# A new instruction order for attention followed by an MLP: planner with margins, last pair's shared tile first, block 8 ahead of blocks 6 and 7, small additions on ScalarE

## The chip, the cores and the metric

The kernel runs on one NeuronCore of a Trainium2 chip. Its engines work through queues of their own, in order: PE (TensorE: matmuls, with weight loads on PEld), DVE (VectorE), ACT (ScalarE), POOL (GpSimd), and SP, which here only issues DMAs, transposes among them. An engine waits for others through semaphores. The metric is the device time of one execution in microseconds (us), lower is better; a time is the median of several runs.

## The reference

Attention with pooled queries over 4 batches x 8 heads, 1152 keys and 576 queries (pairs of neighbours averaged), head size 64; then an MLP over the 2304 rows of 512 features.

```python
q_pool = q.reshape(B, H, S // 2, 2, D).mean(axis=3)
scores = (1 / np.sqrt(D)) * q_pool @ k.transpose(0, 1, 3, 2)
attn = np.exp(scores - scores.max(axis=-1, keepdims=True))
attn = attn / (attn.sum(axis=-1, keepdims=True) + 1e-09)
x = (attn @ v).transpose(0, 2, 1, 3).reshape(B * S // 2, H * D)
h = x @ w_in
out = (h * (1 / (1 + np.exp(-1.702 * h)))) @ w_out
```

q, k and v arrive as 32-bit floats, the weights in double precision. Where the kernel works in f16, it splits an operand into a high and a low f16 part, so that one product becomes three f16 matmuls (high x high, high x low, low x high).

## The kernel before

Heads are worked on in 16 pairs, four to a batch. Each pair has nine tiles of scores (128 queries x 1152 keys): A0, A1, B0, B1, A2, A3, B2, B3 of its two heads, and a shared tile L that holds the last 64 queries of both. Tiles are numbered through, 0 to 143. The first four pairs (tiles 0 to 35) are worked on in 32-bit floats: PE transposes the exponentials (`w_tr`) and ACT or DVE evacuates them (`w_ev`). The other twelve run in f16, and these steps follow one another for a tile:

- `scores` on PE into the one score tile in PSUM (`s`, three banks, one buffer);
- `row_max` on DVE: negated copy into `p` (3 buffers) and row minimum `nm`;
- `lift` on DVE: adds 15 ln 2 to `nm` (so that the f16 parts don't underflow);
- `exps` on ACT: exp with bias `nm`, and the row sums into `w_d`;
- `p_hi` on ACT or DVE: f16 copy of `p` into `hl` (3 buffers);
- `p_lo` on POOL or DVE: the rest, `p` minus that copy;
- `p_tr` on SP: a DMA transpose of both parts into `pt`.

When the four tiles of a group (two of each head), or L, are there, `pv` on PE multiplies by v; `w_denom` on POOL adds 1e-9 to the sums, `w_recip` on DVE inverts, `w_rows` on PE and `w_spread` (ACT or DVE) spread them, `x_div` on DVE multiplies, `x_hi` and `x_lo` split the result for the MLP. A pair's q, k and v go through their own steps ahead (`q_add` on POOL, maxima, `q_hi`, `q_lo`, `k_hi`, `k_lo`, `v_hi`, `v_lo`, two transposes on SP). The weights are unpacked from double precision (`w_exp`, `w_low`, `w_bits`, `w_sign`, `w_mul`, then `w_hi`, `w_lo`) during the first pairs.

The MLP works in nine blocks of 256 rows: two to a batch (0 to 7) of the tiles A and B, and block 8 of the remaining rows, the L tiles of all pairs, prepared by `last_scale`, `last_hi` and `last_lo`. A block has eight steps: `moe_h` in four pieces of six matmuls (an "h piece") into one PSUM buffer, `moe_tanh` on ACT, `moe_gate` on DVE, `moe_hi` on ACT or DVE, `moe_lo` on DVE, and `moe_o` in four pieces of three matmuls (an "o piece"). A block ends with two evacuations (`out_ev` on ACT) and stores on SP.

The order in which instructions stand on the engines is made by a planner (class `Plan`): each task has an engine or several to choose from (`or_on`, by the table `movable`), a cost in us, a rank, and buffers that it takes and gives back. `order` goes through a simulated time; for each engine it looks for the tasks that can start within `wait` of the earliest one and takes that with the lowest rank. The numbers in `rank`, `wait` and `sizes` are set by hand in the source. What it emits stands as it is: an engine whose next instruction waits does nothing else. Tasks marked `two`, and POOL's, are kept apart by the planner (`lock`): they don't overlap in its time.

Of the kernel before, what the change touches and what calls it, by code (L numbers as in the profile page):

```python
# [23 lines left out]
class Plan:  # L24
# [12 lines left out]
    def __init__(self, sizes, wait):  # L37
        self.sizes, self.wait, self.tasks, self.users, self.takers = sizes, wait, [], {}, {}
# [22 lines left out]
    def order(self):  # L61
# [14 lines left out]
        def start(t, e):  # L76
# [4 lines left out]
            for tag, _ in t["take"]:  # L81
# [3 lines left out]
                if at >= 0:  # L85
                    key = held[at]
                    if pend[key]:
                        return None
                    s = max(s, ended[key])
            return s  # L90

        while len(out) < len(self.tasks):
# [13 lines left out]
            cost = t["on"][eng]  # L106
            if eng == "PE":
                cost += self.SWITCH * (t["mode"] != mode)
                mode = t["mode"]
# [16 lines left out]
            for h in heirs.get(t["name"], ()):  # L126
                for e in h["on"]:
                    at = free[e] if e == eng and (e == "PE" or h["name"][0] == t["name"][0]) else seen
# [10 lines left out]
def kernel(  # L139
# [45 lines left out]
        w1=1971.8069114113, w1_rate=22.2436521906, w2=2562.6136217615, w2_rate=0.1126475672,  # L185
        w1_cut=2729.3607183991, w1_cut_rate=0.2375636551, w2_cut=-194.4633781393, w2_cut_rate=0.0258145275,
        v_max=410.1342476678, load=-538.8306800934, prep=169.5826065521, max=-1414.4144022325,
        exp=-771.055026078, p_hi=-369.4985057232, p_lo=318.2880489272, pv=1732.7584590916, x=1798.622401704,
        recip=1777.4431451824, w_tr=1309.6396350423, w_ev=935.5365655987, g=-1469.0890297392,
        pv_b=-864.4518785428, max_b=1888.3689951722, p_lo_b=1106.2277461912, prep_b=-1313.6605845069,  # L190
        v=1427.6770251219, lift=-747.0450393382,
    )
    movable = dict(DVE=('x_hi', 'p_hi', 'x', 'w_hi', 'k_hi', 'moe_hi', 'q_hi', 'qk_ev'), POOL=('p_lo', 'w_exp'))
    wait = dict(PE=0.005839, ACT=0.318681, DVE=0.098398, POOL=1.168057)
# [4 lines left out]
    plan = Plan(sizes, wait)  # L199
# [25 lines left out]
    i_l = const.tile([128, 1], F32, name="i_l")  # L225

# [162 lines left out]
    ORDER = SLOTS  # L389
    pairs, tile_of, num = [], [], {}  # L390
    for P in range(NPAIR):
        pairs.append(Pair(P, len(tile_of), ORDER))
        for kind, t in ORDER:
# [290 lines left out]
    def w_denom(g, u):  # L684
        c = w_cols(g, u)
        nc.gpsimd.tensor_scalar(
            out=w_r[:, c], in0=w_d[:, c], scalar1=1e-9 * (1 if g.whole else 2 ** LIFT), scalar2=1.0, op0=ALU.add, op1=ALU.mult
# [6 lines left out]
    def lift(e, n):  # L694

        m = T["nm", n]
        (nc.vector if e == "DVE" else nc.gpsimd).tensor_scalar(  # L697
# [432 lines left out]
```

## Time and profile before

| | us |
|---|---|
| median of 3 runs (820.05 to 821.11) | 820.67 |
| the profiled execution | 818.89 |
| its span, first to last instruction | 817.1 |
| PE busy / DVE / ACT / POOL | 771.6 / 614.7 / 526.0 / 318.5 |

PE is busy 94% of the span, DVE 75%, ACT 64%, POOL 39%. The page cuts the span into 40 slices of some 20 us; a digit is the busy share in tenths:

```profile
PE   6999999999889898998899999998989999999997
DVE  5786999889999898887989698989788783222222
ACT  5887888988567776686578675656666753222222
POOL 3432334355536455353436664527564530000000
```

Three stages are seen: the first four pairs (to about slice 8), the twelve f16 pairs with MLP blocks between them, and from slice 34 on MLP blocks alone. An idle time of an engine is written behind an instruction with what ended it ("<-"), and a wait for several semaphores is put down to the one that came last.

### The profile page before, as it was taken

How to read it: one execution, taken by the hardware profiler on the slowest of the kernel's cores; microseconds unless marked ns; L12 is line 12 of the kernel's file. 1: busy time of each engine (PE TensorE's matmuls, PEld its weight loads, DVE VectorE, ACT ScalarE, POOL GpSimd, SP SyncE). 2: the span in 40 equal slices, each digit the busy share in tenths (PEclk: the TensorE clock that was granted, in tenths of full speed). 3: DMA queues.
4: the chain of work that ended last, by engine and by line, in shares of the span. 5: the costliest groups of instructions: out<-in, count | busy, mean ns of one | idle time of the engine just before them, and what ended most of it. 6: DMA issues, size and time to landing. Idle time of an engine off the chain costs nothing.

```text
span 817.1 us, 16805 instructions
## 1 busy us (share of the span) xinstructions
PE 771.6 (94%) x6756; PEld 515.6 (63%) x6756; DVE 614.7 (75%) x1053; ACT 526.0 (64%) x787; POOL 318.5 (39%) x235
## 2 busy tenths in 40 slices
PE   6999999999889898998899999998989999999997
PEld 3566666666656566666567666666666667666664
DVE  5786999889999898887989698989788783222222
ACT  5887888988567776686578675656666753222222
POOL 3432334355536455353436664527564530000000
PEclk9999999999999999999999999999999999999999
DMA  8554333769899999999999999999999981000001
GB/s 300 186 173 151 119 125 103 195 125 176 179 176 229 196 205 196 210 195 221 198 206 192 214 204 205 207 215 201 213 182 177 172 139 39 1 27 1 26 1 26
DMA packets 336142, 128.77 MB, mean 158 GB/s; under 512 B 311232, under 2 KB 321472, under 8 KB 336064
## 3 DMA queue, kind: packets, MB, share of 16 engines
q1 hardware_dynamic: 335776, 127.10, 74.6%
q8 instruction: 53, 0.87, 0.4%
q10 hardware_dynamic: 288, 0.59, 0.3%
q14 instruction: 25, 0.20, 0.1%
HBM read 45.09 MB, written 4.72 MB: 61 GB/s over the span
## 4 chain that ended last, share of the span: by engine, by line
PE 62%; DVE 18%; DMA 7%; issue 5%; ACT 4%; SPq 2%; POOL 1%; DVEq 0%; ACTq 0%; POOLq 0%
PE h L951 16%; PE o L987 14%; PE s L654 7%; DMA pt<-hl 6%; DVE p L668 5%; PE s L625 5%; PE pv L733 5%; PE o L745 5%; PE pv L768 5%; DVE kn L497 2%; PE h L308 2%; PE tr L780 2%; DVE hl L254 1%; ACT hl L252 1%; DVE hl L707 1%
## 5 line engine op out<-in xcount | busy, mean ns | idle before, releaser
L707 POOL TENSOR_TENSOR hl<-p,hl 128x1152 f16<-128x1152 f32 x85 | 210.6, 2480 | 186.1 <-ACT hl L252 121.5
L668 DVE TENSOR_SCALAR_CACHE_REDUCE p<-s,e_s 128x1152 f32<-128x1152 f32 x144 | 203.2, 1411 | 41.4 <-PE s L654 15.9
L675 ACT ACTIVATE p<-p,nm 128x1152 f32<-128x1152 f32 x144 | 180.0, 1250 | 56.8 <-DVE nm L697 41.5
L987 PE MATMUL o<-wbuf,g 128*128 128x512 f16 x864 | 205.1, 380 | 0.0
L951 PEld LDWEIGHTS <-wbuf 128*128 128x128 f16 x1728 | 167.5, 98 | 44.7 <-issue 10.1
L654 PE MATMUL s<-kT,qT 128*128 128x384 f16 (+1 forms) x720 | 125.6, 330 | 15.8 <-DVE p L668 15.8
L987 PEld LDWEIGHTS <-g 128*128 128x128 f16 x864 | 82.6, 98 | 85.6 <-issue 3.3
L252 ACT ACTIVATE hl<-p 128x1152 f16<-128x1152 f32 x84 | 97.1, 1157 | 40.6 <-DMA pt<-hl 29.8
L951 PE MATMUL h<-x16a,wbuf 128*128 128x256 f16 x960 | 118.5, 275 | 4.8 <-DVE gf L965 4.7
L959 ACT ACTIVATE th<-h,t_s 128x512 f32<-128x512 f32 x72 | 49.2, 684 | 103.9 <-PE h L951 103.7
L965 DVE SCALAR_TENSOR_TENSOR gf<-th,h 128x512 f32<-128x512 f32 x72 | 49.2, 683 | 85.6 <-ACT th L959 85.5
L654 PEld LDWEIGHTS <-qT 128*128 128x128 f16 (+1 forms) x720 | 63.2, 101 | 63.1 <-issue 25.9
L733 PEld LDWEIGHTS <-vhl 128*64 128x64 f16 x1944 | 80.9, 111 | 21.0 <-issue 17.3
L951 PE MATMUL h<-wbuf 128*128 128x256 f16 x768 | 91.9, 274 | 0.0
L733 PE MATMUL pv<-pt,vhl 128*64 128x256 f16 x1296 | 78.4, 274 | 2.0 <-DMA pt<-hl 2.0
L976 DVE SCALAR_TENSOR_TENSOR g<-gf,g 128x512 f16<-128x512 f32 x72 | 64.3, 894 | 20.0 <-ACT g L252 19.8
L252 ACT ACTIVATE g<-gf 128x512 f16<-128x512 f32 x55 | 34.4, 626 | 33.3 <-DVE gf L965 33.3
L303 POOL TENSOR_TENSOR wbuf<-raw 128x512 f32<-128x512 f32 x32 | 34.1, 1070 | 44.8 <-ACT raw L299 42.8
L745 PE MATMUL o<-idf,p 128*128 128x128 f32 x324 | 50.3, 283 | 0.4 <-ACT pt L252 0.2
L625 PE MATMUL s<-kT,qT 64*128 64x512 f32 (+3 forms) x240 | 49.3, 522 | 0.2 <-DVE p L668 0.2
L252 ACT ACTIVATE pt<-o 128x384 f32<-128x384 f32 x96 | 43.4, 483 | 8.8 <-PE o L745 8.2
L745 PEld LDWEIGHTS o<-idf,p 128*128 128x128 f32 x324 | 35.9, 141 | 17.9 <-issue 6.2
(104 smaller groups left out, 810.0 us busy)
## 6 DMA issues: line engine op xcount, KB each, us to landing
vraw<-in_v_dram SPq DMA_DIRECT2D x32, 288.0 KB, 3.4
kraw<-in_k_dram SPq DMA_DIRECT2D x30, 288.0 KB, 3.5
qraw<-in_q_dram SPq DMA_DIRECT2D x32, 256.0 KB, 4.0
raw<-in_moe_w_in_dram SPq DMA_DIRECT2D x16, 512.0 KB, 4.6
raw<-in_moe_w_out_dram SPq DMA_DIRECT2D x16, 512.0 KB, 4.8
out_dram<-osb SPq DMA_DIRECT2D x16, 256.0 KB, 2.7
pt<-hl SPq DMA_TRANSPOSE x96, 5.1
qraw<-in_q_dram SPq DMA_DIRECT2D x32, 32.0 KB, 3.6
```

What stands on the lines that cost most here:

```text
L252: nc.scalar.activation(out=out, in_=in_, func=ACTF.Copy, scale=1.0 if scale is None else scale)
L625: nc.tensor.matmul(out=ps[m, bank, 0:128 * (last - first)], lhsT=qT[h, (j - half) % NJ, m], rhs=kT[h, first:last].rearrange("p j c -> p (j ...
L654: nc.tensor.matmul(out=ps[m, c, 0:384], lhsT=st, rhs=T["kT", g.P][:, o:o + 3].rearrange("p r c -> p (r c)"), start=(l == 0), stop=(l == 1),)
L668: nc.vector.tensor_scalar(out=p, in0=s, scalar1=e_s[:, g.P:g.P + 1], scalar2=None, op0=ALU.mult, op1=ALU.min, accum_out=m)
L675: nc.scalar.activation(out=p, in_=p, func=ACTF.Exp, bias=T["nm", n], scale=-1.0, accum_out=sm)
L707: (nc.vector if e == "DVE" else nc.gpsimd).tensor_tensor(out=t[:, 1, :], in0=T["p", n].rearrange("p c f -> p (c f)"), in1=t[:, 0, :], op=A ...
L733: nc.tensor.matmul(out=ps[64 * a:64 * (a + 1), 0:w], lhsT=T["vhl", g.P][:, a, g.block[a][c], m], rhs=pt[:, l * KR + c, o:o + w], start=(pa ...
L745: nc.tensor.transpose(ps[:, 128 * i:128 * (i + 1)], T["p", n][:, c, 128 * i:128 * (i + 1)], idf)
L951: nc.tensor.matmul(out=h[:, e, :], lhsT=w1(2 * j + e, l, kk), rhs=x_rhs(blk, m, kk), start=(kk == 0 and l == 0 and m == 0), stop=(kk == KD ...
L959: nc.scalar.activation(out=t, in_=T["h", blk, j].rearrange("p e n -> p (e n)"), func=ACTF.Tanh, scale=t_s[:, b:b + 1])
L976: nc.vector.scalar_tensor_tensor(out=g[:, 1].rearrange("p e n -> p (e n)"), in0=T["gf", blk, j], scalar=2.0 ** -16, in1=g[:, 0].rearrange( ...
L987: nc.tensor.matmul(out=o, lhsT=g[:, l, e, 128 * t:128 * (t + 1)], rhs=w2(fc, m), start=(fc == 0 and l == 0 and m == 0), stop=(fc == KFF - ...
```

## The change

- The planner gets a table `slack`. A task on PE may start `slack["PE"]` (0.298 us) after what it waits for, or after a buffer is given back, is seen; costs of the other engines are multiplied (ACT 1.03, DVE 1.02, POOL 1.20, SP 1.08).
- `rank`, `movable` and `wait` have other numbers. `p_hi`, `x_hi`, `moe_hi`, `w_spread`, `w_exp` and `q_hi` can no longer go to DVE or POOL and stay on ACT; `v_hi`, `x_even` can go to DVE.
- `lift` (108 instructions) goes from DVE to ACT, `w_denom` (48) from POOL to ACT, both as an Identity ACTIVATE whose bias is a column of a new tile `add_c`, set by three memsets on DVE at the start.
- The last pair's order of tiles begins with L (it is tile 135; A0 to B3 are 136 to 143).
- Block 8 comes ahead of blocks 6 and 7. What is computed doesn't change.

```diff
-            s = max(s, ended[key])
+            s = max(s, ended[key] + (self.slack["PE"] if e == "PE" else 0.0))
...
             cost = t["on"][eng]
+            if eng != "PE":
+                cost *= self.slack[eng]
...
-    at = free[e] if e == eng and (e == "PE" or h["name"][0] == t["name"][0]) else seen
+    at = free[e] if e == eng and (e == "PE" or h["name"][0] == t["name"][0]) else seen + (self.slack["PE"] if e == "PE" else 0.0)
...
-        w1=1971.8069114113, w1_rate=22.2436521906, ...
+        w1=1635.4577871165, w1_rate=0.1876384407, ...
...
-    movable = dict(DVE=('x_hi', 'p_hi', 'x', 'w_hi', 'k_hi', 'moe_hi', 'q_hi', 'qk_ev'), POOL=('p_lo', 'w_exp'))
-    wait = dict(PE=0.005839, ACT=0.318681, DVE=0.098398, POOL=1.168057)
+    movable = dict(DVE=('qk_ev', 'w_hi', 'k_hi', 'v_hi', 'x_even', 'w_sign'), POOL=('p_lo', 'denom'))
+    wait = dict(PE=0.073718, ACT=0.133022, DVE=0.295657, POOL=0.285145)
+    slack = dict(PE=0.297637, ACT=1.031989, DVE=1.023033, POOL=1.19561, SP=1.076504)
...
-    ORDER = SLOTS
+    ORDERS = [SLOTS] * (NPAIR - 1) + [SLOTS[-1:] + SLOTS[:-1]]
...
-        nc.gpsimd.tensor_scalar(
-            out=w_r[:, c], in0=w_d[:, c], scalar1=1e-9 * (1 if g.whole else 2 ** LIFT), scalar2=1.0, op0=ALU.add, op1=ALU.mult
+        i = 1 if g.whole else 2
+        nc.scalar.activation(
+            out=w_r[:, c], in_=w_d[:, c], func=ACTF.Identity, bias=add_c[:, i:i + 1], scale=1.0
         )
...
-        (nc.vector if e == "DVE" else nc.gpsimd).tensor_scalar(
-            out=m, in0=m, scalar1=LIFT * math.log(2.0), scalar2=1.0, op0=ALU.add, op1=ALU.mult
-        )
+        if e == "DVE":
+            nc.vector.tensor_scalar(out=m, in0=m, scalar1=LIFT * math.log(2.0), scalar2=None, op0=ALU.add)
+        else:
+            nc.scalar.activation(out=m, in_=m, func=ACTF.Identity, bias=add_c[:, 0:1], scale=1.0)
...
-    for blk in range(2 * B + 1):
+    for blk in list(range(2 * B - 2)) + [2 * B, 2 * B - 2, 2 * B - 1]:
```

Two more lines mark `x_hi` and `moe_hi` with `two=True`.

How the change moves instructions is shown at three places. The first is DVE at tiles 108 to 110, in the middle of the f16 pairs. `row_max` is the row whose results are `p,nm`; `nm<-nm` is the lift, `CAST hl<-p` is `p_hi`, `CAST x16a` is `x_hi`, `gf` is the gate and `g<-gf,g` is `moe_lo`. Before, from the lift of tile 108 on:

```order
L697 TENSOR_SCALAR nm<-nm 128x1
L254 CAST x16a<-xf 128x256
L254 CAST hl<-p 128x1152
L668 TENSOR_SCALAR p,nm<-s,e_s 128x1152
L697 TENSOR_SCALAR nm<-nm 128x1
L965 SCALAR_TENSOR_TENSOR gf<-th,h 128x512
L254 CAST hl<-p 128x1152
L668 TENSOR_SCALAR p,nm<-s,e_s 128x1152
```

Now, from the maximum of k that follows `row_max` of tile 108:

```order
L435 TENSOR_REDUCE qkv<-kraw 128x1
L971 SCALAR_TENSOR_TENSOR gf<-th,h 128x512
L672 TENSOR_SCALAR p,nm<-s,e_s 128x1152
L982 SCALAR_TENSOR_TENSOR g<-gf,g 128x512
L697 RECIPROCAL w_r<-w_r 128x1
L672 TENSOR_SCALAR p,nm<-s,e_s 128x1152
L971 SCALAR_TENSOR_TENSOR gf<-th,h 128x512
```

A `p_hi` stood directly ahead of each of these two `row_max`; now a gate and a reciprocal do, and the lifts are gone.

The second is ACT at the same tiles. `p,w_d<-p,nm` is the exp, `th` is the tanh, `osb` an evacuation of a block's result. Before, from the exp of tile 108 on:

```order
L675 ACTIVATE p,w_d<-p,nm 128x1152
L959 ACTIVATE th<-h,t_s 128x512
L675 ACTIVATE p,w_d<-p,nm 128x1152
L252 ACTIVATE g<-gf 128x512
L675 ACTIVATE p,w_d<-p,nm 128x1152
L252 ACTIVATE hl<-p 128x1152
```

Now, from the lift of tile 108 on:

```order
L705 ACTIVATE nm<-nm,add_c 128x1
L691 ACTIVATE w_r<-w_d,add_c 128x1
L679 ACTIVATE p,w_d<-p,nm 128x1152
L256 ACTIVATE g<-gf 128x512
L1001 ACTIVATE osb<-o_5526,o_s 128x512
L705 ACTIVATE nm<-nm,add_c 128x1
L256 ACTIVATE hl<-p 128x1152
L679 ACTIVATE p,w_d<-p,nm 128x1152
L965 ACTIVATE th<-h,t_s 128x512
```

Each exp has its lift on its own engine ahead of it, with a denominator or a `p_hi` between, and all `p_hi` of the stage stand here.

The third is SP at the last pair. `DMA_TRANSPOSE pt<-hl` is `p_tr` of a tile, `ptl` that of an L tile; `DMA out_dram` stores a block's rows, four of 64 rows for block 8. Before, from the transposed k of the last pair on:

```order
L504 DMA_TRANSPOSE kT<-kn 128x18x128
L1002 DMA out_dram<-osb 128x512 x2
L720 DMA_TRANSPOSE pt<-hl 128x18x128 x5
L720 DMA_TRANSPOSE ptl<-hl 128x18x128
L720 DMA_TRANSPOSE pt<-hl 128x18x128 x8
L720 DMA_TRANSPOSE ptl<-hl 128x18x128
L1002 DMA out_dram<-osb 128x512 x6
L1006 DMA out_dram<-osb 64x512 x4
```

Now:

```order
L508 DMA_TRANSPOSE kT<-kn 128x18x128
L726 DMA_TRANSPOSE pt<-hl 128x18x128 x6
L726 DMA_TRANSPOSE ptl<-hl 128x18x128 x2
L726 DMA_TRANSPOSE pt<-hl 128x18x128 x3
L1008 DMA out_dram<-osb 128x512
L726 DMA_TRANSPOSE pt<-hl 128x18x128 x2
L1008 DMA out_dram<-osb 128x512
L726 DMA_TRANSPOSE pt<-hl 128x18x128 x3
L1012 DMA out_dram<-osb 64x512 x4
L1008 DMA out_dram<-osb 128x512 x4
```

The last pair's L tile follows the previous pair's directly, the stores of block 5 stand among the transposes of the last tiles, and block 8 is stored ahead of blocks 6 and 7. On PE, 498 h and 264 o matmuls stand behind the last pv instruction, where 600 and 315 stood.

## Rows read from the trace of the kernel before

**Rows 1.** Stretches: bounds, length, busy us (instructions) of PE, PEld, DVE, ACT, POOL.

```profile
20.00:160.00 140.00, 139.02 (x1021) 85.90 (x1023) 116.72 (x219) 121.75 (x225) 52.82 (x60) 1.00 0.47 149
160.00:680.00 520.00, 487.21 (x4779) 333.64 (x4772) 449.84 (x765) 356.57 (x489) 257.82 (x161) 0.99 1.01 192
680.00:817.10 137.10, 132.59 (x909) 88.58 (x907) 37.05 (x54) 36.92 (x56) 0.00 (x0) 0.99 0.05 16
```

**Rows 2.** Waits of PE, 160 to 680: us in total, times, longest.

```profile
PE s L654 <- DVE p L668: 15.8, 17, 2.4
PE h L951 <- DVE gf L965: 4.7, 3, 2.1
PE pv L733 <- DVE xf L810: 4.5, 2, 2.5
```

**Rows 3.** Timeline around three waits of PE: start, length, instruction, [idle before <- cause].

```profile
173.89 2.30 DVE L256 TENSOR_SCALAR wbuf<-wbuf,s_w 128x1024 f16<-128x1024 f32 x1
...
176.70 0.51 PE L768 MATMUL pv<-ptl,vraw 128*64 128x64 f32 x10 [1.10 <-DVE xf L812]
...
229.99 1.41 DVE L497 SCALAR_TENSOR_TENSOR kn<-kraw,s_qkv,kn 128x1152 f16<-128x1152 f32 x1
...
565.11 6.12 POOL L707 TENSOR_TENSOR hl<-p,hl 128x1152 f16<-128x1152 f32 x2 [0.18 <-POOL wbuf L824]
565.47 3.53 DVE L497 SCALAR_TENSOR_TENSOR kn<-kraw,s_qkv,kn 128x1152 f16<-128x1152 f32 x1
...
570.39 0.81 PE L654 MATMUL s<-kT,qT 128*128 128x384 f16 x4 [2.39 <-DVE p L668]
...
657.41 2.86 DVE L976 SCALAR_TENSOR_TENSOR g<-gf,g 128x512 f16<-128x512 f32 x1
...
661.66 0.65 PE L654 MATMUL s<-kT,qT 128*64 128x384 f16 x5 [1.75 <-DVE p L668]
```

**Rows 4.** Timeline: a cast on DVE that waits for a buffer, and PE.

```profile
549.57 0.76 DVE L254 CAST hl<-p 128x1152 f16<-128x1152 f32 x1 [1.27 <-DMA pt<-hl]
...
551.72 0.65 PE L654 MATMUL s<-kT,qT 128*128 128x384 f16 x3 [1.39 <-DVE p L668]
```

**Rows 5.** Groups of the whole span: shapes, count | busy us, mean ns | idle before.

```profile
L675 ACT ACTIVATE p<-p,nm 128x1152 f32<-128x1152 f32 x144 | 180.0, 1250 | 56.8 <-DVE nm L697 41.5 <-DVE p L668 5.3 <-DVE w_r L692 4.6
L252 ACT ACTIVATE hl<-p 128x1152 f16<-128x1152 f32 x84 | 97.1, 1157 | 40.6 <-DMA pt<-hl 29.8 <-issue 5.3 <-DMA ptl<-hl 4.4
L252 ACT ACTIVATE g<-gf 128x512 f16<-128x512 f32 x55 | 34.4, 626 | 33.3 <-DVE gf L965 33.3
L697 DVE TENSOR_SCALAR nm<-nm 128x1 f32<-128x1 f32 x108 | 15.9, 148 | 1.2
L252 ACT ACTIVATE raw<-raw 128x512 f32<-128x512 f32 x19 | 13.0, 687 | 0.2 <-DMA raw<-in_moe_w_out_dram 0.2
```

**Rows 6.** What touches `hl`: count, ns least/median/most, first and last start.

```profile
L720 SPq DMA_TRANSPOSE pt<-hl x96: 2402/3254/4547, 172.8 to 667.0; - x96
L707 POOL TENSOR_TENSOR hl<-p,hl x85: 2365/2377/3555, 170.4 to 664.6; 128x1152 f16<-128x1152 f32 x85
```

**Rows 7.** Timeline of the start, up to the first scores.

```profile
8.81 0.60 ACT L252 ACTIVATE qT<-o 128x512 f32<-128x512 f32 x1 [2.75 <-PE o L518]
...
9.59 0.69 DVE L293 SCALAR_TENSOR_TENSOR raw<-raw 128x512 int32<-128x512 int32 x1 [0.54 <-POOL raw L285]
...
10.71 0.51 PEld L625 LDWEIGHTS s<-kT,qT 64*128 64x128 f32 x4 [0.33 <-issue]
```

**Rows 8.** The chain that ended last, and the timeline, at the end.

```profile
804.69 2.62 PE h L951 x24
807.31 5.30 PE o L987 x24
...
812.05 2.46 SPq L1006 DMA_DIRECT2D out_dram<-osb  x4
```

**Rows 9.** The gate on DVE, 160 to 680: as rows 5.

```profile
L965 DVE SCALAR_TENSOR_TENSOR gf<-th,h 128x512 f32<-128x512 f32 x47 | 32.0, 681 | 8.4 <-ACT th L959 8.3
```

## Prediction before the run

> **What bounds the kernel now.** I read the stretches first, then the waits of PE, then the timeline around the waits. PE is busy 771.6 us of the 817.1 us span. Until 160 us (the first four pairs, which work in 32-bit floats) it idles under 1 us in 140, and from 680 us on, where only MLP blocks are left, only at the very end; in the stage between, 160 to 680 us, it is busy 487.2 of 520 us [rows 1]. These 32.8 us of idle PE are what an order can win back. In that stage DVE is busy 449.8 us (87%), ACT 356.6 (69%), POOL 257.8 (50%). The longest waits of PE there all end with DVE: scores wait for `row_max` to free the one score tile (17 times, 15.8 us), `moe_h` for the gate (4.7), pv for `x_div` (4.5) [rows 2].
>
> Why DVE is late is seen in the timeline. `k_lo` of one pair takes 1.41 us; of another, behind a POOL `p_lo`, 3.53 us; `row_max` stands behind it and PE idles 2.39 us [rows 3]. I went through the 20 idle times of PE over 0.6 us in the stage (28.9 us in all): 15 of them, 24.2 us, begin behind a DVE instruction drawn out in this way; the first is a `w_hi` of 2.30 us (1.10 us of idle PE), the last a `g_lo` of 2.86 us (1.75) [rows 3]. In two more (2.1 us together, the second shown) DVE stood at a `p_hi` whose `hl` buffer a transpose had not given back, with `row_max` queued behind it [rows 4].
>
> **The change, part by part.** The sum is made against the profiled execution, 818.9 us (span 817.1 and 1.8 around it); the median of the three timed runs is 1.8 us more.
>
> *Work off DVE and POOL.* All `p_hi` (24 had been on DVE), `x_hi` (19), `moe_hi` (17), `w_spread` (18) and the 108 lifts now go to ACT, and 10 `p_lo` go from POOL to DVE. PE doesn't see DVE's sum, only late instructions. Of those that can be drawn out (they read and write SBUF alone), the new order has 135 on DVE between the first and the last f16 tile, the old one 169; POOL loses 10 `p_lo` of 2.38 us [rows 6], 9% of its 257.8 us (its 48 small additions go too, not counted). If meetings go with the product of the two, 0.80 x 0.91 = 0.73 of them stay: 24.2 x 0.27 = 6.6 us saved. Bounds: nothing (the long `k_lo` and `g_lo` all stay), and 24.2. The two waits at `p_hi` leave DVE with it: 2.1 us.
>
> *Planner's margins.* PE's next piece is now chosen as if what it waits for came 0.3 us later, and POOL's work is counted 20% longer. So more work stands on PE ahead of a piece whose input is close. Rows 2 count 22 waits; 0.3 us off each is 6.6 us. Bounds: nothing, and all that is left of the 32.8 us.
>
> *Block of the remaining rows.* The last pair's shared tile comes first, so that block 8 can run while blocks 6 and 7 wait for that pair. By itself this saves no work: four h pieces take 2.62 us and eight o pieces 5.30 us [rows 8], in either place. It gives PE something to do earlier. Behind the last pv instruction PE had 600 h and 315 o instructions, now 498 and 264: 17 pieces of each, 17 x 0.655 + 17 x 0.66 = 22.4 us, have gone into the stage. This is the cover for the margins. If the stage grows by 22.4 us, nothing is won; by my sum it grows by about 9 (32.8 less 15.3 of idle time, and 22.4 more work, make 527 us of the old 520, and the slower start comes on top). Block 8 adds a wait: its first h piece needs last_lo, which needs the last pair's shared rows. Six o pieces and two scores, some 6 us, stand on PE between that pair's shared pv and this piece; `x_div`, last_hi and last_lo behind each other are about half of it, so I count nothing; if the cover failed, some 3 us. On SP the two stores of block 5 now stand among the last pair's transposes, and a transpose queued behind a store would wait for its evacuation, and pv for it; the o pieces that this evacuation needs stand some 8 us of PE work behind the scores of the tile whose transpose follows, and that tile needs about as long to get there: nothing, or again some 3 us.
>
> *Lift and 1e-9 on ACT.* A one-column ACTIVATE with a bias tile isn't in the trace. Exp with a bias tile takes 1.250 us for 1152 columns, plain copies 1.157 for 1152 and 0.626 for 512 [rows 5]. The copies differ by 0.83 ns a column, so one column would be about 0.29 us with the bias, 0.20 without; these are the bounds, and I take 0.29, whose row has the bias: 108 lifts 31 us, 48 denominators 14. On DVE the lift was 0.15 [rows 5], behind whatever stood there. Each lift waits for `row_max`; behind it on ACT stand the exp of the same tile, and tanh and evacuations, for which DVE's gate and then PE wait. ACT waited for the lifted value before too, so the place of the wait moves rather than its end: nothing. The denominators wait for exps of their own engine: nothing.
>
> *ACT's load.* In the stage 24 `p_hi` x 1.157 = 27.8, 14 `moe_hi` x 0.626 = 8.8, some 26 small copies at about 0.37 = 10, and lifts with denominators 42, less 3 `v_hi`: about 85 us more, 441 of 520, 85%: what DVE carries now.
>
> *First four pairs.* All 32 `w_exp` are on ACT (13 came from POOL, 0.69 us each [rows 5], 9 us) with 4 or 5 us of small pieces. ACT is at 121.8 of 140 us there [rows 1], so this still fits; between nothing and 14 us I take 2, nearer to nothing, since PE stands idle under 1 us of the 140 with ACT at 87%.
>
> *Start.* The evacuations of the first q and k go from ACT to DVE, with `w_low` and `w_bits` (0.69) between. Before, ACT took the first q from 8.81 us on and scores began at 10.71 [rows 7]. With a `w_bits` in the row, plus 0.7 us; bounds 0 and 1.4. *End.* One store of 256 KB follows the last evacuation in place of the last two of four, issued from 812.05 us on over 2.46 us [rows 8]: minus 0.4, bounds minus 1 and 0.
>
> Sum: -6.6 - 2.1 - 6.6 + 2.0 + 0.7 - 0.4 = **-13.0 us**, or 805.9 us for an execution like the profiled one, 807.7 beside the median.
>
> **The rivals.** *Nearly all idle time goes.* If margins and the lighter DVE took 28 of the 32.8 us, the time would be 820.7 - 28 + 2.3 = 795. Against it: SP issues 132 transposes, nearly all in this stage, of some 3.2 us each [rows 6], about 420 us, and the loads; the less PE idles, the faster SP must go.
>
> *Nothing is won.* Meetings of POOL and DVE hang on where an execution drifts, not on the plan; the long `g_lo`, `k_lo` and `p_lo` stay on DVE, and 10 more `p_lo`. Then the stage grows by the 22.4 us of work put into it: 820.7 + 2.3 - 2.1 = 821, within a us or two of before. The page "SBUF — State Buffer" of the Trainium skill (SBUF: two separate sides) says that DVE operations with two SBUF inputs or in a two-port mode and GpSimd operations lock each other out for a whole instruction. By that rule a margin of 0.3 us is no help against a meeting that costs 2 us; the 3.53 us `k_lo` agrees with it.
>
> *Slower: ACT becomes what DVE was.* With 85% on ACT, each lift stands in order between a late `row_max` and the tanh behind it. If ACT sets the pace, the stage grows by the lifts' 31 us and the moved work isn't covered: 820.7 + 31 - 13 = about 839; it decides from where ACT is busy over some 95% of the stage. For it: 156 tiny instructions at twice DVE's price. Against it: in the first stage PE idles under 1 us though ACT is at 87% [rows 1]. The page "ScalarE: Activation LUTs" (Rules for kernel authors) speaks against the change: additions belong on VectorE. The same page's figure of 280 ns and 0.83 ns a column for an ACTIVATE with a bias pointer would give the lifts 30 us, as the rows do.
>
> **How the numbers follow.** The forecast, half of the idle time gone: 0.57, 800 to 818 us. Nearly all gone: 0.15, 790 to 800. Nothing won: 0.12, 819 to 823. ACT-bound: 0.16, 823 to 840. A measurement of this kernel can tell 0.2%, 1.6 us: faster by more 0.57 + 0.15 + 0.02 = 0.74, within 0.08, slower 0.02 + 0.16 = 0.18. The range from 794 to 824 leaves out the lower part of the second case and most of the last, somewhat under 0.2.
>
> **What would show it.** Right: PE idle in the stage at 15 to 20 us; waits of scores for `row_max` under 10 us; last pv near 688 us (now near 679); ACT's busy share in the stage near 85%, DVE's near 78%; fewer drawn-out DVE instructions ahead of `row_max`. Wrong: as many drawn-out instructions and as much idle PE, with the last pv past 701 us (no gain); gates waiting for tanh, now 8.3 us in the stage [rows 9], at 25 or more (ACT-bound); PE waiting for evacuations before 160 us; block 8 waiting for last_lo. If PE idles under 8 us in the stage, my share of meetings was too cautious.

## The result, and the profile after

The changed kernel takes 799.83 us (median of 4 runs, 798.88 to 802.39) where the kernel before, on the same chip, took 820.36 (4 runs, 818.98 to 821.11): 0.9762 of it, 95% interval 0.9734 to 0.979. The profiled execution took 798.88 us with a span of 797.1; before it was 818.9 and 817.1. Three executions of the runs further down were far longer than the rest of their kernels (883, 985 and 1554 us) and are left out of the ratios.

The stretches of the changed kernel, with the columns of [rows 1] (bounds, length, busy us of PE, PEld, DVE, ACT, POOL, then the granted clock, the DMA share and GB/s):

```profile
20.00:160.00 140.00, 136.48 (x996) 83.61 (x997) 111.05 (x198) 125.97 (x252) 37.45 (x37) 1.00 0.42 145
160.00:680.00 520.00, 505.06 (x4920) 347.76 (x4918) 412.96 (x620) 432.99 (x714) 226.19 (x115) 1.00 1.03 194
680.00:797.10 117.10, 113.50 (x798) 76.07 (x794) 29.50 (x43) 31.97 (x49) 0.67 (x1) 1.00 0.05 14
```

Beside [rows 1]: in the stage from 160 to 680 us PE idles 14.9 us instead of 32.8. DVE went from 449.8 to 413.0 us, ACT from 356.6 to 433.0 (83% of the stage), POOL from 257.8 to 226.2. The first stage pays: idle PE there grew from 1.0 to 3.5 us. Over the whole span PE is busy 767.6 us (771.6 before) and idle 29.5 (45.5): 16.0 of the 20.0 us are idle time, 4.0 are shorter work.

The waits of PE from 160 to 680 us, as in [rows 2]:

```profile
PE s L658 <- DVE p L672: 2.7, 5, 0.9
PE pv L739 <- DMA pt<-hl: 2.4, 3, 1.4
PE h L957 <- DVE gf L971: 2.4, 2, 1.6
```

Scores waiting for `row_max` were 17 waits and 15.8 us; 5 and 2.7 us are left. Waits of the other engines in the same stretch show who waits instead:

```profile
DVE p L672 <- PE s L658: 31.1, 38, 2.1
...
ACT hl L256 <- DMA pt<-hl: 18.7, 14, 2.9
...
DVE gf L971 <- ACT th L965: 17.0, 17, 3.8
```

`row_max` now stands ready for its scores 38 times (31.1 us; 18 times and 15.9 us before). For each of the 108 tiles of the stage I took from the instruction records how long after its last score matmul `row_max` began: 1.47 us on the mean before, 0.80 now (over 1 us late 47 times before, 28 times now). Of the work that PE has between two tiles' scores, 17 gaps held under 2 us before, 6 now; the mean rose from 3.18 to 3.34.

**Where the 20 us lie.** Scores end at the same time, 662.8 us before and 663.2 now; the last pv ends at 678.9 and 682.0. Behind it stand 138.2 us before and 115.1 now, since 102 h and 51 o matmuls of PE fewer are left, by the order. So 23.1 us of MLP work went into a stage that grew by 3.1.

### The profile page after: what moved, and what is told of

Its sections match the earlier page's. It is cut to its first block, busy times and chain, and to the rows that moved or that the text cites. A ratio compares the mean times of both kernels' runs of the same rounds, so it can differ in the third digit from the quotient of the medians.

```text
span 797.1 us, 16744 instructions
## 1 busy us (share of the span) xinstructions
PE 767.6 (96%) x6756; PEld 514.8 (65%) x6756; DVE 564.4 (71%) x883; ACT 601.5 (75%) x1031; POOL 270.1 (34%) x164
## 4 chain that ended last, share of the span: by engine, by line
PE 59%; DVE 13%; DMA 10%; ACT 7%; issue 6%; POOL 2%; SPq 2%; DVEq 0%; POOLq 0%; ACTq 0%
PE o L993 16%; PE h L957 15%; PE s L658 8%; PE pv L739 8%; DMA pt<-hl 5%; DVE p L672 4%; PE s L629 3%; PE pv L774 3%; PE o L751 3%; DMA ptl<-hl 3%; ACT p L679 2%; ACT hl L256 2%; DMA raw<-in_moe_w_in_dram 2%; PE tr L786 2%; DVE wbuf L330 1%
## 5 line engine op out<-in xcount | busy, mean ns | idle before, releaser
L713 POOL TENSOR_TENSOR hl<-p,hl 128x1152 f16<-128x1152 f32 x75 | 186.3, 2487 | 209.1 <-ACT hl L256 167.5
L672 DVE TENSOR_SCALAR_CACHE_REDUCE p<-s,e_s 128x1152 f32<-128x1152 f32 x144 | 203.5, 1413 | 52.7 <-PE s L658 31.1
L256 ACT ACTIVATE hl<-p 128x1152 f16<-128x1152 f32 x108 | 124.8, 1156 | 25.5 <-DMA pt<-hl 18.7
L658 PE MATMUL s<-kT,qT 128*128 128x384 f16 (+1 forms) x720 | 123.9, 327 | 2.8 <-DVE p L672 2.7
L739 PEld LDWEIGHTS <-vhl 128*64 128x64 f16 x1944 | 80.6, 111 | 15.9 <-issue 8.5
L739 PE MATMUL pv<-pt,vhl 128*64 128x256 f16 x1296 | 76.1, 273 | 2.4 <-DMA pt<-hl 2.4
L982 DVE SCALAR_TENSOR_TENSOR g<-gf,g 128x512 f16<-128x512 f32 x72 | 59.0, 819 | 17.3 <-ACT g L256 17.1
L256 ACT ACTIVATE g<-gf 128x512 f16<-128x512 f32 x72 | 44.7, 621 | 18.5 <-DVE gf L971 18.5
L713 DVE TENSOR_TENSOR hl<-p,hl 128x1152 f16<-128x1152 f32 x33 | 45.7, 1386 | 12.2 <-ACT hl L256 11.7
```

The costliest lines, as they stand in the source:

```text
L256: nc.scalar.activation(out=out, in_=in_, func=ACTF.Copy, scale=1.0 if scale is None else scale)
L658: nc.tensor.matmul(out=ps[m, c, 0:384], lhsT=st, rhs=T["kT", g.P][:, o:o + 3].rearrange("p r c -> p (r c)"), start=(l == 0), stop=(l == 1),)
L672: nc.vector.tensor_scalar(out=p, in0=s, scalar1=e_s[:, g.P:g.P + 1], scalar2=None, op0=ALU.mult, op1=ALU.min, accum_out=m)
L713: (nc.vector if e == "DVE" else nc.gpsimd).tensor_tensor(out=t[:, 1, :], in0=T["p", n].rearrange("p c f -> p (c f)"), in1=t[:, 0, :], op=A ...
L739: nc.tensor.matmul(out=ps[64 * a:64 * (a + 1), 0:w], lhsT=T["vhl", g.P][:, a, g.block[a][c], m], rhs=pt[:, l * KR + c, o:o + w], start=(pa ...
L982: nc.vector.scalar_tensor_tensor(out=g[:, 1].rearrange("p e n -> p (e n)"), in0=T["gf", blk, j], scalar=2.0 ** -16, in1=g[:, 0].rearrange( ...
```

## The experiments

Each ratio is to the kernel before on the same chip. The undoing runs carry on from 0.9762. Where an edit says "in its order", every other instruction keeps its place, and no planner runs anew. "Drawn out" is the sum, over DVE's instructions from 160 to 690 us, of what each took above the shortest tenth of its form.

| kernel | ratio, 95% | idle PE in 160:680 | scores wait for row_max | row_max behind scores, mean | drawn out |
|---|---|---|---|---|---|
| before | 1 | 32.8 us | 15.8 us, 17 | 1.47 us | 51.7 us |
| changed | 0.9762 (0.9734 to 0.979) | 14.9 | 2.7, 5 | 0.80 | 27.5 |
| e1 | 1.0041 (1.002 to 1.0062) | 32.2 | 18.6, 21 | 1.57 | 33.2 |
| e2 | 0.9983 (0.996 to 1.0006) | 33.9 | 17.7, 19 | 1.57 | 49.7 |
| e3 | 1.0184 (1.0123 to 1.0246) | 33.2 | 17.4, 12 | 1.33 | 46.3 |
| e4 | 0.991 (0.9881 to 0.9939) | 26.4 | 17.2, 22 | 1.50 | 24.3 |
| e5 | 0.988 (0.9841 to 0.992) | 23.0 | 7.4, 6 | 0.98 | 41.4 |
| e6 | 0.9994 (0.9975 to 1.0013) | 30.3 | 4.2, 8 | 0.87 | 27.7 |
| e7 | 1.0399 (1.0362 to 1.0436) | 52.5 | 27.0, 20 | 1.12 | 25.1 |
| e8 | 0.9847 (0.982 to 0.9874) | 21.4 | 3.1, 6 | 0.83 | 32.0 |
| e9 | 0.9808 (0.9765 to 0.9852) | 19.2 | 2.9, 7 | 0.83 | 34.7 |
| e10 | 0.9709 (0.9673 to 0.9746) | 12.6 | 2.0, 3 | 0.65 | 8.3 |
| e11 | 0.989 (0.986 to 0.992) | 21.2 | 13.3, 10 | 0.97 | 32.2 |
| e12 | 0.9848 (0.9813 to 0.9884) | 19.6 | 2.6, 5 | 0.79 | 27.3 |

**e1: the casts from DVE to ACT, old order.**

```diff
         for t, e in plan.order():
+            if t["name"][0] in ("H", "x_hi", "g_hi"):
+                e = "ACT"
             t["fn"](e) if t["free"] else t["fn"]()
```

> The kernel before, every instruction in its old order, with one edit: the p_hi (24), x_hi (19) and moe_hi (17) that its planner had put on DVE are issued on ACT. Nothing else of the change: old block order, no margins, lifts on DVE, denominators on POOL. My theory (a lighter DVE is one part of the gain: no CAST of DVE waits for an hl buffer, fewer instructions there can be drawn out): 4 to 6 us faster than before, about 815, with the two stalls of rows 4 gone and PE idle in the stage from 160 to 680 us at 27 to 29 us (32.8 before). Rival (the planner's new order is what wins; work taken from DVE without a new order is worth nothing): within 1.5 us of 820. Rival (ACT carries the pace): slower, 823 or more, with gates waiting for tanh by 20 us or more.

DVE lost 40 us of work in the stage and nothing was won; it is 0.4% slower. The same place in both timelines (start, length, engine and line, [idle before <- cause]) shows how. Kernel before, the tile 131 of 144:

```profile
615.41 0.75 DVE L254 CAST hl<-p 128x1152 f16<-128x1152 f32 x1
...
615.80 0.62 ACT L252 ACTIVATE g<-gf 128x512 f16<-128x512 f32 x1
...
616.45 2.72 DVE L976 SCALAR_TENSOR_TENSOR g<-gf,g 128x512 f16<-128x512 f32 x1 [0.28 <-ACT g L252]
...
619.09 1.40 DVE L668 TENSOR_SCALAR_CACHE_REDUCE p<-s,e_s 128x1152 f32<-128x1152 f32 x1
...
620.56 1.14 PE L654 MATMUL s<-kT,qT 128*128 128x384 f16 x6 [1.47 <-DVE p L668]
```

e1, the same tile:

```profile
614.59 1.15 ACT L252 ACTIVATE hl<-p 128x1152 f16<-128x1152 f32 x1
...
615.64 0.62 ACT L252 ACTIVATE g<-gf 128x512 f16<-128x512 f32 x1
...
616.29 2.49 DVE L976 SCALAR_TENSOR_TENSOR g<-gf,g 128x512 f16<-128x512 f32 x1 [2.17 <-ACT g L252]
...
618.71 1.41 DVE L668 TENSOR_SCALAR_CACHE_REDUCE p<-s,e_s 128x1152 f32<-128x1152 f32 x1
...
620.17 1.14 PE L654 MATMUL s<-kT,qT 128*128 128x384 f16 x6 [3.22 <-DVE p L668]
```

The cast is gone from DVE, but `moe_lo`, next in DVE's order and ahead of `row_max`, now waits 2.17 us (0.28 before) for an ACT instruction that stands behind that cast. PE idles 3.22 us for `row_max` where it idled 1.47. Over the stage the waits of e1 read:

```profile
ACT hl L252 <- DMA pt<-hl: 40.7, 30, 4.1
...
DVE gf L965 <- ACT th L959: 25.6, 19, 2.7
...
DVE g L976 <- ACT g L252: 18.3, 18, 2.2
```

In the kernel before these were 29.8, 8.3 and 4.4 us. The wait for the `hl` buffer moved from DVE to ACT, and `tanh` and `moe_hi`, queued behind it there, passed it back to DVE. `row_max` itself also waited longer for a `p` buffer that `p_lo` on POOL gives back (14.1 us, 6.6 before).

**e2: the block order alone** in the kernel before, planned anew; only the last pair's part of the order changes.

```diff
-    ORDER = SLOTS
+    ORDERS = [SLOTS] * (NPAIR - 1) + [SLOTS[-1:] + SLOTS[:-1]]
...
-    for blk in range(2 * B + 1):
+    for blk in list(range(2 * B - 2)) + [2 * B, 2 * B - 2, 2 * B - 1]:
```

> The kernel before with only the block order of the change: the last pair's shared tile first, and block 8 before blocks 6 and 7, planned anew with the old ranks, costs and no margins. Only the order from the last pair on differs. My theory (the block ahead saves no work by itself; the idle time of the stage stays): 0 to 3 us faster, 817 to 820, PE idle in the stage 30 us or more, the end about 0.4 us shorter by the single store. Rival (the 22.4 us of MLP work moved ahead of the last pv are themselves what fills the idle time): 806 or less, PE idle in the stage under 22 us.

0.9983, an interval that reaches 1: the theory holds. 18 h and 3 o matmuls more than before run ahead of the last pv; idle PE in the stage stays (33.9 us).

**e3: the margins alone**, in the old ranks, planned anew.

```diff
+    slack = dict(PE=0.297637, ACT=1.031989, DVE=1.023033, POOL=1.19561, SP=1.076504)
-    plan = Plan(sizes, wait)
+    plan = Plan(sizes, wait, slack)
```

> The kernel before with only the margins of the change in its planner (PE's next piece chosen as if what it waits for came 0.298 us later, POOL's work counted 20% longer, and the rest of that table), planned anew with the old ranks. Old block order, lifts on DVE. My theory (0.3 us off each of 22 waits of PE): 6 us faster, 812 to 816, PE idle in the stage 24 to 28 us. Rival (margins of 0.3 us don't help against meetings of 2 us, and the old ranks were chosen for an order without margins): 819 or more, PE idle in the stage 31 us or more, as many waits of scores for row_max as before (17).

Slower by 1.8%, as the rival had it, with idle PE in the stage at 33.2 us. There are fewer waits for `row_max` (12 for 17) and gaps under 2 us are 8 for 17, so the margins do fill gaps; but the waits that are left are as long together (17.4 us). The span is 14.5 us longer: 3.7 more idle PE before 160 us, 0.7 from there to the last scores, 3.7 between the last scores and the last pv (none before), and 6.4 of longer busy PE (778.0 us), whose cause is open.

**e4: POOL's p_lo without reading**, in the order of before.

```diff
-        (nc.vector if e == "DVE" else nc.gpsimd).tensor_tensor(
...
+        if e == "DVE":
+            nc.vector.tensor_tensor(
...
+        else:
+            nc.gpsimd.memset(t[:, 1, :], 0.0)
+            nc.gpsimd.memset(t[:, 1, :], 0.0)
```

> The kernel before in its old order, with POOL's p_lo (85) replaced by two writes of zeros of the same buffer, about as long together as the subtraction: POOL then reads nothing, the low half of p is left out for the tiles of POOL, and the time is that of the same work on all other engines. My theory (PE's stalls come from DVE instructions drawn out next to POOL's p_lo): the k_lo of 3.5 us, g_lo of 2.9 and w_hi of 2.3 shrink to their usual lengths, PE idle in the stage falls from 32.8 to 10 to 15 us, time 797 to 803. Rival (the long DVE instructions have another cause, or POOL's writes draw them out just as its subtraction does): as many drawn-out instructions (26 in the stage, 52 us together), PE idle 30 us or more, 817 to 821.

The mechanism is there. `k_lo` over 160 to 690 us (least/median/most ns), in the kernel before, in e4 and in the changed kernel:

```profile
L497 DVE SCALAR_TENSOR_TENSOR kn<-kraw,s_qkv,kn x11: 1403/1411/3530, 194.0 to 609.4; 128x1152 f16<-128x1152 f32 x11
```

```profile
L497 DVE SCALAR_TENSOR_TENSOR kn<-kraw,s_qkv,kn x11: 1404/1412/1419, 192.2 to 602.7; 128x1152 f16<-128x1152 f32 x11
```

```profile
L501 DVE SCALAR_TENSOR_TENSOR kn<-kraw,s_qkv,kn x11: 1405/1409/1821, 193.9 to 604.4; 128x1152 f16<-128x1152 f32 x11
```

Not one `k_lo` is drawn out in e4. The Trainium skill's page "SBUF — State Buffer" (SBUF: two separate sides) has it so: a DVE operation with two SBUF inputs is locked out only by a GpSimd operation that reads SBUF; the trace agrees. All of DVE's lengthening fell from 51.7 to 24.3 us. But the time fell by 7.4 us only, not by 17 to 23, and idle PE by 6.4.

That is 0.27 us for each us of lengthening, but it is no clean price, because the edit changed two more things. The writes of zeros read neither `p` nor its copy, so they no longer wait for `p_hi`. In the kernel before, POOL stood 43.9 us for the `p_hi` of DVE and, for those of ACT,

```profile
POOL hl L707 <- ACT hl L252: 121.5, 45, 8.2
```

and in e4 both waits are gone: a transpose now waits for the longer of the two steps, not for both in turn. And the writes can run beside the `p_hi` of their own tile, which then is drawn out in its turn. The `p_hi` on DVE in the kernel before and in e4 (least/median/most ns), and one of them in e4:

```profile
L254 DVE CAST hl<-p x24: 730/760/2884, 234.1 to 638.8; 128x1152 f16<-128x1152 f32 x24
```

```profile
L254 DVE CAST hl<-p x24: 753/1329/1715, 230.1 to 634.3; 128x1152 f16<-128x1152 f32 x24
```

```profile
546.11 1.69 DVE L254 CAST hl<-p 128x1152 f16<-128x1152 f32 x1 [1.40 <-DMA pt<-hl]
546.13 1.06 POOL L712 MEMSET hl<- 128x1152 f16 x1 [0.60 <-DMA pt<-hl]
...
549.18 0.48 PE L654 MATMUL s<-kT,qT 128*128 128x384 f16 x2 [2.31 <-DVE p L668]
```

The lengthening of these casts grew from 4.6 to 11.2 us, and two of e4's three longest waits of PE (2.72 and 2.31 us) come behind such a cast. So the theory was right on what draws out `k_lo`, and wrong on the time; what the lengthening costs by itself stays open.

**e5: the counterpart of e1.** The changed kernel in its order, with the 60 casts of e1 back on DVE.

```diff
         for t, e in plan.order():
+            if t["name"] in on_dve:
+                e = "DVE"
             t["fn"](e) if t["free"] else t["fn"]()
```

> The changed kernel, every instruction in its order, with those 24 p_hi, 19 x_hi and 17 moe_hi that the kernel before had on DVE put back on DVE. It is the counterpart of e1, where the same 60 went to ACT in the old order and nothing was won. Theory from e1 (where these copies run is worth little; what counts is which instructions the order puts on DVE ahead of row_max): 0.976 to 0.984 of before, row_max starting on average 0.8 to 1.1 us after the end of its scores in the stage (1.47 before, 0.80 in the changed kernel). Rival (the lighter DVE is what the new order lives on): 0.990 or more, row_max 1.3 us or more behind its scores.

0.988, between the two: about half of the gain goes (1.2% of 820, 9.7 us). `row_max` comes 0.98 us behind its scores, so the order keeps most of that; drawn-out time returns to 41.4 us. The same move that won nothing in the old order is worth half the gain in the new one.

**e6: block 8 to the very end**, all else in the changed kernel's order.

```diff
+        last = [x for x in plan_order if of_last(x[0]["name"])]
-        for t, e in plan.order():
+        for t, e in [x for x in plan_order if not of_last(x[0]["name"])] + last:
```

> The changed kernel in its order, with all instructions of block 8 taken out of their places and put at the very end, behind blocks 6 and 7, as the kernel before has them; nothing else is moved. In the changed kernel 13 h and 8 o pieces of block 8, 21 x 0.66 = 13.8 us of PE, stand ahead of the last pv. Theory (block 8 is the cover of the last pair; e2 showed that without a new order it alone gives little, 0 to 0.4%): PE idles about as long as these pieces took, 8 to 14 us, between 630 and 690 us, so 0.986 to 0.993 of before. Rival (other pieces already cover the last pair, block 8's place is worth nothing): 0.975 to 0.979, no more idle PE there.

The whole gain is gone (0.9994), more than the 8 to 14 us of the theory. Scores end at 663.5 us as in the changed kernel (663.2), but PE has done less by then (4.7 us more idle time since 160 us), and the rest is lost behind them. The timeline of e6 there (`pt<-hl` on SP are the transposes of the last tiles):

```profile
666.25 3.13 PE L739 MATMUL pv<-pt,vhl 128*64 128x256 f16 x53 [2.52 <-DMA pt<-hl]
...
667.60 9.24 SPq L726 DMA_TRANSPOSE pt<-hl  x3
...
671.96 0.66 PE L786 MATMUL tr<-idf,w_r 128*64 128x128 f32 x8 [2.13 <-DVE w_r L697]
```

And PE alone, further on:

```profile
678.90 4.62 PE L739 MATMUL pv<-pt,vhl 128*64 128x256 f16 x53 [6.03 <-DMA pt<-hl]
683.45 2.79 PE L957 MATMUL h<-wbuf 128*128 128x256 f16 x24
687.75 2.78 PE L957 MATMUL h<-wbuf 128*128 128x256 f16 x24 [1.50 <-DVE gf L971]
```

In the changed kernel the same stretch has no wait, and the last pv runs at its usual pace:

```profile
678.07 0.82 PE L957 MATMUL h<-x16a,wbuf 128*128 128x256 f16 x6
678.82 3.14 PE L739 MATMUL pv<-pt,vhl 128*64 128x256 f16 x54
681.88 2.14 PE L957 MATMUL h<-x16a,wbuf 128*128 128x256 f16 x18
```

Between the last scores and the last pv stands a chain (exp, `p_hi`, `p_lo`, three transposes of some 3 us one behind another). Blocks 0 to 5 are used up by then, so with block 8 gone PE idles 10.7 us there, 4.0 more than the changed kernel behind the last pv, and works some of it at a lower clock (below).

**e7: the margins out of the changed kernel**, planned anew.

```diff
-    slack = dict(PE=0.297637, ACT=1.031989, DVE=1.023033, POOL=1.19561, SP=1.076504)
+    slack = dict(PE=0.0, ACT=1.0, DVE=1.0, POOL=1.0, SP=1.0)
```

> The changed kernel planned anew with its ranks, but with the planner's margins at nothing (0 us for PE, factor 1 for the rest). e3 gave margins to the old ranks and lost 1.8%: more was lost in the first 160 us and behind 680 us, and scores waited as long as before. Theory (the margins do their work together with the ranks: PE has more other work between two scores; of 108 gaps 6 are filled with under 2 us, 17 before): idle PE in the stage grows from 14.9 to 21 to 30 us, 0.983 to 0.993 of before. Rival (the ranks alone carry the gain, margins nothing): 0.974 to 0.979, idle PE at 18 us or less.

4% slower than before, far past the theory's 0.983 to 0.993: 42 of 107 gaps hold under 2 us (6 in the changed kernel), idle PE is 52.5 us, and PE's busy time is 784.5 us at a mean granted clock of 0.976 (767.6 and 0.998). A loss of 4% is more than any margin of 0.3 us a wait could give, which made me doubt that this run measures the margin; e11 is the control.

**e8 and e9: the lift back on DVE**, in the changed kernel's order; e8 puts the 48 additions of 1e-9 back on POOL as well.

```diff
+            if t["name"][0] == "B":
+                lift("DVE", t["name"][1])
+                continue
             t["fn"](e) if t["free"] else t["fn"]()
```

> The changed kernel in its order, with the 108 lifts put back on DVE and the 48 additions of 1e-9 back on POOL. Theory of the prediction (where the lift runs is worth nothing, the wait only changes its place): 0.974 to 0.980 of before. Rival (each lift on DVE stands ahead of other work of DVE and is a part of the delay): 0.981 or more. Rival (the lift of 0.28 us on ACT delays the exps and through them the kernel): 0.972 or less.

> The changed kernel in its order, with only the 108 lifts back on DVE; the 48 additions of 1e-9 stay on ACT. e8, which put both back, lost 0.85% where the prediction had counted nothing; there w_recip waited for POOL (the transposes of xt stood 5.0 us for w_recip, 1.7 before) and gates had grown. Theory (the loss of e8 is the denominators on POOL, behind its p_lo): 0.974 to 0.979 of before, waits for w_recip under 2 us. Rival (the loss is the lift: 0.14 us of DVE ahead of each exp and of what is queued on DVE): 0.982 to 0.987, waits for w_recip under 2 us all the same.

Both together cost 0.85% (0.9847, interval apart from the changed kernel's). The lift alone stands at 0.9808, with an interval that overlaps both: its own worth, some 4 us, is not settled, and neither is that of the additions (e8 and e9 overlap). For the additions the trace has a place: `w_recip` (L697) waits for POOL in e8,

```profile
DVE w_r L697 <- POOL w_r L691: 11.1, 8, 3.5
```

while in the changed kernel it waits for ACT:

```profile
DVE w_r L697 <- ACT w_r L691: 3.9, 3, 2.8
```

The addition itself is about as short on either engine; but in those eight waits it stands on POOL right behind a `p_lo` (four times) or a `q_add` (four times). The expected fall of PE's wait for `w_recip` below 2 us in e9 did not come (2.8 us on the x transposes).

**e10: e4's edit in the changed kernel's order** (the diff is that of e4).

> The changed kernel in its order, with its 75 p_lo on POOL replaced by two writes of zeros of the same buffer, as e4 did with the kernel before: the low half of p is left out for POOL's tiles. In the kernel before this took 28 us off the drawn-out DVE instructions and 7.4 us (0.9%) off the time. Theory (the same meetings cost the changed kernel less, since it has 15 drawn-out instructions where before had 26, and fuller gaps between scores): 0.970 to 0.975 of before, that is 1 to 5 us below the changed kernel. Rival (the meetings still cost what they did): 0.965 to 0.968, 7 us or more below. Rival (nothing more to win there): 0.975 to 0.979.

0.9709, 0.5% or 4.4 us below the changed kernel, as the theory had it, though the two intervals overlap (0.9734 to 0.9746). 27.5 us of drawn-out time became 8.3, 0.23 us for each; here too POOL no longer waits for `p_hi` (167.5 us for that of ACT in the changed kernel), so this is no clean price either. It leaves out part of p, so it is a bound and no kernel to use.

**e11: one number moved by 4%.**

```diff
-    slack = dict(PE=0.297637, ACT=1.031989, DVE=1.023033, POOL=1.19561, SP=1.076504)
+    slack = dict(PE=0.310000, ACT=1.031989, DVE=1.023033, POOL=1.19561, SP=1.076504)
```

> The changed kernel planned anew with one number moved by 4%: PE's margin 0.310 us in place of 0.298; nothing else. A control for e3 and e7, which planned anew with numbers that were fitted to other margins. Theory (ranks and margins are fitted to each other, and any other number gives an order that is not fitted, so that e3 and e7 tell of the fit and not of the margin): 0.983 to 1.000 of before, with more idle PE in the stage than the 14.9 us of the changed kernel. Rival (time follows the margin smoothly, and e7's 4% is what the margin is worth): 0.974 to 0.979.

0.989: 1.3% lost to a margin that is 12 ns longer. Waits for `row_max` are back at 13.3 us, although the gaps between scores are as full as in the changed kernel (6 under 2 us, 3.34 on the mean): full gaps alone do not keep scores from waiting. So a new plan with numbers that were not fitted to it can cost of itself as much as most of the parts in dispute; one such step was run. e3 and e7, and e12 as well, tell of that fit and cannot be read as the price of the part that they changed.

**e12: block 8 last, planned anew.** The diff of e2 the other way round, in the changed kernel:

```diff
-    for blk in list(range(2 * B - 2)) + [2 * B, 2 * B - 2, 2 * B - 1]:
+    for blk in range(2 * B + 1):
```

> The changed kernel planned anew with the block order and the pair order of before (block 8 last, the last pair's shared tile last), all its other numbers kept. e6 moved block 8 without a new plan and lost the whole gain: PE stood 10.7 us between the last scores and the last pv with nothing else to do. Theory (without block 8 the planner has only blocks 0 to 5 to fill the gaps of sixteen pairs; whatever it keeps back for the last pair it lacks earlier): 0.990 to 1.005. Rival (the planner makes up for it from other blocks, block 8 is worth little once the order is planned for it): 0.974 to 0.982.

0.9848, above the rival's range and below the theory's: two thirds of the gain stay. With the shared tile last, the rows of block 6 are done earlier, and the new plan puts four h pieces of block 6 and two o pieces of block 5 among the last tiles (idle PE between the last scores and the last pv is 3.0 us, 10.7 in e6). What is lost, 0.9%, is no more than what e11 lost by a nudge, so e12 does not show that the gain needs block 8; e6 shows that this order needs it.

No run beat the changed kernel with the whole computation done. Undone one at a time in its order, the casts (e5), block 8 (e6) and the small additions (e8) cost 9.7, 19.0 and 7.0 us, 36 us of a gain of 20: the parts lean on one another, and their prices can't be added up.

## Why the prediction was right, and where its terms were off

807.7 us was predicted, 799.8 came; faster was the likeliest case, and the range (794 to 824) holds it. The measured time stands on the border between the likeliest stretch (800 to 818) and the next one (790 to 800). Step by step:

- **Idle PE in the stage.** Predicted 32.8 less 15.3, 17.5 left; measured 14.9. It lies at the edge of the sign (15 to 20); that of scores waiting under 10 us (2.7) came. The mechanism of the forecast is the one seen: `row_max` is ready earlier (0.80 us behind its scores, 1.47 before) and PE has somewhat more other work between scores (3.34 us, 3.18 before). By e11 the second alone is not enough.
- **Work off DVE, -6.6.** The size fits, the reasoning doesn't, and the fit is luck. It took 24.2 us of idle time as caused by the drawn-out instructions ahead of it, and let 0.73 of them stay. In fact 0.53 of the lengthening stayed (27.5 / 51.7; what went is 24.2 us, the same figure by chance), and with the rough ratio of e4 this is worth 24.2 x 0.27 = 6.5. Too little was expected to go, and too much was expected of it. That a stall begins behind a long instruction does not make the whole stall its price: e4 took 27.4 us of lengthening away and still had 22 waits for `row_max`, some of them behind casts that its own writes drew out. The true price is open.
- **The two waits at p_hi, -2.1.** Taken out by hand in e1, they came back as DVE's waits for ACT. As a separate term it is not shown. "PE doesn't see DVE's sum, only late instructions" is what e1 shows at its purest: 40 us off DVE, nothing won.
- **Margins, -6.6.** Not separable: e3, e7 and e11 change the fit as well. Gaps under 2 us went from 17 to 6 in the changed kernel and to 8 in e3, so margins do put work between scores, as was said of them; their price stays open.
- **Block 8.** "By itself this saves no work" (e2) and "the cover" (e6) both hold, and the feared waits for last_lo and for SP's stores did not come: PE has no wait of 0.3 us or more between 620 us and the end of its work. The last pv was forecast near 688 us and came at 682.0.
- **Lift and 1e-9.** The unit price was right: 0.29 us predicted, and the lifts of the changed kernel (count | busy us, mean ns | idle before) have

```profile
L705 ACT ACTIVATE nm<-nm,add_c 128x1 f32<-128x1 f32 x108 | 30.8, 286 | 17.2 <-DVE p L672 16.8
```

  The Trainium skill's page "ScalarE: Activation LUTs" (What ACT_TABLE_LOAD costs) states 280 ns and 0.83 ns a column for an ACTIVATE with a bias pointer, and the trace agrees. "Nothing" for its place was too low for the pair of them: 0.85% (e8). A term that the sum lacked is POOL's 48 additions, "not counted" there: on POOL they stand behind `p_lo` and `q_add`, and `w_recip` waits for them (11.1 us in e8). How the 0.85% divides between them and the lifts is open.
- **ACT-bound.** ACT at 83% (85% predicted), and gates wait 17.0 us for `tanh`, twice the 8.3 of [rows 9] but under the 25 of that rival. PE's own wait for the gate fell from 4.7 to 2.4 us. The Trainium skill's rule on the page "ScalarE: Activation LUTs" (Rules for kernel authors), additions belong on VectorE, holds here for the price of one (0.15 us on DVE, 0.29 on ACT) and not for the kernel: e9 follows it for the lifts and is not faster than the changed kernel.
- **First stage, start and end.** Predicted +2.0, +0.7, -0.4; measured idle +2.5, +0.2, -0.9.
- **What was missing: the clock, some 3.4 us.** The sum had no term for it. PE's busy time fell from 771.6 to 767.6 us with the same instructions; the granted clock fell less often, a mean of 0.998 over the span for 0.992. Three falls of the kernel before show it, each right behind 2.1 to 2.5 us of idle PE:

```profile
320.00:324.00 4.00, 4.00 (x21) 2.60 (x19) 2.76 (x5) 3.61 (x5) 0.23 (x1) 0.58 1.13 207
```

```profile
400.00:404.00 4.00, 3.36 (x65) 2.34 (x65) 3.53 (x7) 2.19 (x4) 0.67 (x1) 0.73 1.14 212
404.00:408.00 4.00, 4.00 (x22) 2.28 (x21) 2.69 (x5) 2.96 (x4) 2.54 (x2) 0.84 1.02 201
```

```profile
604.00:608.00 4.00, 2.10 (x57) 1.46 (x57) 3.93 (x10) 1.60 (x3) 2.69 (x2) 0.83 1.04 223
608.00:612.00 4.00, 4.00 (x26) 2.58 (x24) 3.97 (x6) 3.55 (x4) 0.57 (x1) 0.74 0.82 156
```

  In the changed kernel no wait of PE in the stage is over 1.61 us, and there is one fall:

```profile
188.00:192.00 4.00, 3.16 (x16) 2.00 (x15) 3.90 (x11) 3.63 (x6) 2.79 (x2) 0.69 0.76 173
192.00:196.00 4.00, 4.00 (x28) 2.66 (x28) 4.00 (x6) 4.00 (x7) 0.72 (x1) 0.88 0.90 171
```

  What the clock lacks of 1.00 in these stretches, times their 4 us, is 5.1 us before and 1.7 now: 3.4 of the 4.0. The repeated timings of the kernel before agree in size. Of its 44 on three chips, the five with a mean granted clock of 1.000 took 814.4 to 817.0 us, the five at 0.992 or less 817.9 to 821.6. So a full clock is worth some 4 us at most to the kernel before, and the rest of the 20 is not the clock's. The miss of 7 us (-20.0 against -13.0) is 4.0 of shorter busy time, 2.6 more idle time won in the stage, and half a us at the end.

## What to carry to other kernels

Before moving work off a busy in-order engine, look at what stands behind that work on both engines: e1 turned 40 us of DVE work into waits for ACT, and the same move paid only in an order laid out for it (e5). Price a suspected cause by taking it away in the old order, and look what else went with it (e4 won 7.4 us where 24.2 us of idle time began behind the cause, but its edit also dropped a wait and drew out other instructions). Test a part of a planned order by moving instructions in the finished list, since a new plan with one number 4% off cost 1.3% by itself (e11). At the end of a dependent chain, keep independent work in stock for the engine that will wait there (e6: 19 us).

## What the runs showed of the hardware

A long idle time of PE can cost twice. In e6 PE idled 6.03 us and then ran 53 pv matmuls in 4.62 us, where 54 take 3.14; the stretches around it (granted clock third from the end):

```profile
672.00:676.00 4.00, 0.87 (x9) 0.47 (x9) 0.00 (x0) 0.56 (x2) 0.67 (x1) 0.89 1.49 179
676.00:680.00 4.00, 1.10 (x12) 0.93 (x14) 0.00 (x0) 0.00 (x0) 0.00 (x0) 0.50 0.52 115
680.00:684.00 4.00, 4.00 (x50) 3.45 (x47) 0.37 (x1) 0.00 (x0) 0.00 (x0) 0.75 0.00 0
684.00:688.00 4.00, 2.50 (x24) 2.09 (x22) 0.80 (x2) 1.38 (x3) 0.67 (x1) 1.00 0.00 0
```

From 676 us on the clock is at half, the lower of its two levels (1.2 of 2.4 GHz), and comes back between 680 and 684. I had not expected it to matter in a kernel whose PE is 94% busy: in the kernel before, five waits of PE in the stage were over 2 us long (2.01 to 2.53), and three of them were followed by such a fall. Why the other two were not is open. The length of one wait does not decide it: the changed kernel's fall, from 188 us on, came behind waits of 1.00 and 0.84 us.
